# Placing the weight-decoding steps by the position within an expert in a fused attention, expert and feed-forward kernel

## Chip, core and metric

The kernel runs on one core of one Trainium2 chip, as one launch. The metric is the device time of that launch in microseconds. The engines that matter here are TensorE (matrix products), VectorE and ScalarE (elementwise work), GpSimd (elementwise work and gathers) and SyncE (which issues most of the transfers). Each engine works through its own list of instructions in order and waits at an instruction until what that one needs has arrived.

## What is computed

Three parts, one after the other, on 2304 tokens of width 512, in float32 (the weights of part 3 come in float64):

```python
# 1. attention with a decaying causal mask, 4 x 8 heads, 576 positions, head width 64
ret = scores * Dmat;  x = ret @ v                       # -> [2304, 512]
# 2. eight experts, one per token
expert_idx = argmax(xn @ en.T / tau)                    # one of 8
h = np.maximum(x[mask] @ w1[e], 0.0)                    # [tokens of e, 1024]
out[mask] = gate_w[mask, None] * (h @ w2[e])
# 3. feed-forward, d_ff 2048, weights given in float64
h = x @ w_in
g = np.where(h > 0.0, h, np.exp(np.minimum(h, 0.0)) - 1.0)
return g @ w_out
```

## The kernel before

**Precision.** Every product in parts 2 and 3 is made of three passes. A value is split into a high part `hi` (a rounded copy) and a low part `lo` (the rest), and `three` issues high x high, high x low and low x high.

**Expert loop.** The loop over `i` from 0 to 64 at the end of the listing below does part 2. Expert `e = i // 8` has its 1024 hidden units in eight slices, and `f = i % 8` is the place within the expert. In iteration `i`:

- `mm1(i)`: TensorE multiplies the tokens of the expert with slice `i` of `w1` (12 products). ScalarE then writes `hh`, the high part of the rectified result (L861), and VectorE `hl`, the low part (L862).
- `mm2(i-1)`: TensorE multiplies `hh`, `hl` of the slice before with its slice of `w2` into four accumulators `acc0` to `acc3` (12 products). The second product of the first accumulator reads `hl`. Where `i - 1` was the last slice of an expert, so in the iteration with `f` = 0, the results are taken: ScalarE copies each accumulator to `yh` (L878) and VectorE makes `yl` (L879), four times. The next expert's first `mm2` overwrites the accumulators, so it waits for these.
- for `f` = 4, 5, 6: `xpose` turns the next expert's gathered rows around (TensorE), with a copy on ScalarE (L839) and a subtraction on VectorE (L840).
- `split(i+2)`: the weights of slice `i + 2` are split, `ah` and `bh` on ScalarE (L208), `al` and `bl` on VectorE (L209).
- `decode(n)`: `n` steps of decoding, the subject of the change.

The instructions of each engine stand in this order. For VectorE the list of one iteration is thus: `hl`, then `yl` four times where `f` = 0, then the subtraction of `xpose` where `f` is 4 to 6, then `al` and `bl` for slice `i + 2`, and last the decoding steps. What the steps delay is `hl` of the next iteration and all that stands behind it.

**Decoding.** The weights of part 3 are float64 and are turned into float32 by whole-number arithmetic, in 32 blocks of 128 x 512, in the background of parts 1 and 2 and the start of part 3. A block takes four steps, each one instruction on VectorE: L145, L147, L150, L153. The second also issues a square on ScalarE (L148). The fourth also issues two transfers on SyncE: the load of the block after next, and the store of the finished block to the buffer `wd`. There are two blocks' buffers in turn. `decode(n)` runs the next `n` of the 128 steps, wherever the sequence stands.

**Gathers.** On GpSimd, `gather_expert` fetches the rows of the expert after next as soon as the transposes have freed the row buffers, in three pieces (L806), and multiplies each by its gates (L816, both inputs in on-chip memory).

**Where the steps go.** 12 steps run in part 1. In the expert loop an iteration runs `1 + (i % 3 == 1)` steps, for `i` up to 61: 83 in all. The remaining 33 run in part 3, from its loop over `j` (at most four an iteration).

Of the kernel before, what the change touches and what calls it, by code (L numbers as in the profile page):

```python
# [79 lines left out]
def tile_kernel(ctx: ExitStack, tc: tile.TileContext, q, k, v, emb, tau, w1, w2, w_in, w_out, const, out):  # L80
# [81 lines left out]
    def decode(n):  # L162
        for _ in range(n):
            next(dsteps, None)
# [654 lines left out]
    def gather_expert(e):  # L819
        if e < NE:  # L820
            i_, g_ = (ids0, gsl0) if e == 0 else (idsp[:, e], gslp[:, e])
            gather(e, lambda j: i_[:, j:j + 1], lambda j: g_[:, j:j + 1], e == 0)
# [3 lines left out]
    def xpose(key, j):  # L826
        if key not in rows:
            return
        if j == 0:
            xt[key] = [mp.tile([P, KD, CAPS[0]], F32R, tag=f"xt{a}", name=f"xt{a}_{key}")[:, :, :cap(key)] for a in "hl"]  # L830
        pt = pm.tile([P, KD, P], F32, tag="acc0" if (key, j) == (0, 2) else "tp", name=f"tp{key}_{j}", bufs=1 if (key, j) == (0, 2) else 2)
        o, m = subs(key)[j]
        for kk in range(KD):
            nc.tensor.transpose(pt[:, kk, :m], rows[key][j][:m, kk, :P], ident[:m, :m])
        h_, l_ = (t[:, :, o:o + m] for t in xt[key])
        if (key, j) == (0, 1):
            vec.tensor_copy(out=h_, in_=pt[:, :, :m])
        else:
            nc.scalar.copy(out=h_, in_=pt[:, :, :m])  # L839
        low = lambda: vec.tensor_tensor(out=l_, in0=pt[:, :, :m], in1=h_.bitcast(F32), op=ALU.subtract)  # L840
        if key != 0:
            low()
        return low
# [3 lines left out]
    def mm1(i, key, w):  # L847
        hp = pm.tile([P, 512], F32, tag="h", name=f"h{i}", bufs=2)
        ah, al = w[:2]
        xh, xl = xt[key]  # L850
        c = cap(key)
        if i:
            for kk in range(KD):
                three(hp[:, :c], (ah[:, kk, :], al[:, kk, :]), (xh[:, kk, :], xl[:, kk, :]), kk == 0, kk == KD - 1)
        else:
            for l, r in ((ah, xh), (al, xh), (ah, xl)):
                for kk in range(KD):
                    nc.tensor.matmul(hp[:, :c], l[:, kk, :], r[:, kk, :], start=l is ah and r is xh and kk == 0, stop=r is xl and kk == KD - 1)
        hh = mp.tile([P, CAPS[0]], F32R, tag="hh", name=f"hh{i}")[:, :c]
        hl = mp.tile([P, CAPS[0]], F32R, tag="hl", name=f"hl{i}")[:, :c]  # L860
        nc.scalar.activation(out=hh, in_=hp[:, :c], func=AF.Relu)  # L861
        vec.scalar_tensor_tensor(out=hl, in0=hp[:, :c], scalar=0.0, in1=hh.bitcast(F32), op0=ALU.max, op1=ALU.subtract)  # L862
        hs[i] = (hh, hl)
# [3 lines left out]
    def mm2(i, f, key, w, ra, rv):  # L867
        c = cap(key)
        bh, bl = w[2:]
        if f == 0:  # L870
            for d in range(KD):
                acc[d] = pm.tile([P, 512], F32, tag=f"acc{d}", name=f"acc{i}_{d}")
        for d in range(KD):
            three(acc[d][:, :c], (bh[:, d, :], bl[:, d, :]), hs[i], f == 0, f == 7)
        if f == 7:
            ra, rv = ra(), rv()
            for d in range(KD):
                nc.scalar.copy(out=yh[d][:, bass.ds(ra, c)], in_=acc[d][:, :c])  # L878
                vec.tensor_tensor(out=yl[d][:, bass.ds(rv, c)], in0=acc[d][:, :c],  # L879
                                  in1=yh[d][:, bass.ds(rv, c)].bitcast(F32), op=ALU.subtract)  # L880

    def reg(eng, ap, top):
        return lambda: eng.value_load(ap, min_val=0, max_val=top)
# [11 lines left out]
    def compact():  # L895

        oe = qp.tile([P, NE], F32, name="oe")
        vec.tensor_tensor(out=ord_["t"], in0=ord_["perm"].rearrange("q p e -> q e p"),
                          in1=ord_["off"][:, :NE].unsqueeze(1).to_broadcast([P, NE, NE]), op=ALU.mult)
        vec.tensor_reduce(out=oe, in_=ord_["t"], axis=AX.X, op=ALU.add)  # L900
        t = qp.tile([P, NT, NE], F32, name="po1")
        pos = qp.tile([P, NT], F32, name="pos")
        pool.tensor_tensor(out=oe, in0=oe, in1=C("base"), op=ALU.subtract)
        rf = qp.tile([P, NT], F32, name="rf")
        pool.tensor_copy(out=rf, in_=rk)
        pool.tensor_tensor(out=t, in0=oh, in1=oe.unsqueeze(1).to_broadcast([P, NT, NE]), op=ALU.mult)
        vec.tensor_reduce(out=pos, in_=t, axis=AX.X, op=ALU.add)
        pool.tensor_tensor(out=pos, in0=pos, in1=rf, op=ALU.add)
        posi = qp.tile([P, 2, NT], I32, name="posi")
        posf = qp.tile([P, 2, NT], F32, name="posf")  # L910
        pool.tensor_copy(out=posi[:, 0, :], in_=pos)
        vec.tensor_scalar(out=posi[:, 1, :], in0=posi[:, 0, :], scalar1=127, scalar2=None, op0=ALU.bitwise_and)
        vec.tensor_scalar(out=posi[:, 0, :], in0=posi[:, 0, :], scalar1=7, scalar2=None, op0=ALU.arith_shift_right)
        pool.tensor_copy(out=posf, in_=posi)
        return posf
# [4 lines left out]
    def compact_part(k, posf):  # L920
        bt = qp.tile([P, CK, P], BF16, tag="cb", name=f"cb{k}", bufs=3)
        at = qp.tile([P, CK, NPART, NT], BF16, tag="ca", name=f"ca{k}", bufs=3)
        for j in range(CK):
            n = k * CK + j
            o18 = qp.tile([P, NT], BF16, name=f"co{n}", tag="co", bufs=2)
            pool.tensor_scalar(out=bt[:, j, :], in0=C("i128"), scalar1=posf[:, 1, n:n + 1], scalar2=None, op0=ALU.is_equal)
            pool.tensor_scalar(out=o18, in0=C("i128")[:, :NT], scalar1=posf[:, 0, n:n + 1], scalar2=None, op0=ALU.is_equal)
            pool.tensor_tensor(out=at[:, j], in0=o18.unsqueeze(1).to_broadcast([P, NPART, NT]),
                               in1=parts[:, n, :].unsqueeze(2).to_broadcast([P, NPART, NT]), op=ALU.mult)
        cparts[k] = (bt, at)  # L930

    def compact_sum(k):
        if k == 0:
            cparts["pc"] = pm.tile([P, NPART, NT], F32, tag="tp", name="pc", bufs=2)
        bt, at = cparts[k]
        for j in range(CK):
            n = k * CK + j
            nc.tensor.matmul(cparts["pc"].rearrange("p a b -> p (a b)"), bt[:, j, :], at[:, j].rearrange("p a b -> p (a b)"),
                             start=n == 0, stop=n == NT - 1)

    def compact_end():
        pc = cparts["pc"]
        cid = qp.tile([P, 2, NT], F32, name="cid")
        for j, (lo, hi) in enumerate(((0, 2), (2, NPART))):
            vec.tensor_reduce(out=cid[:, j, :], in_=pc[:, lo:hi].rearrange("p a b -> p b a"), axis=AX.X, op=ALU.add)
        vec.tensor_copy(out=idc, in_=cid[:, 0, :])
        cparts["cid"] = cid
# [62 lines left out]
    for i in range(NI1 + 1):  # L1010
        if i < NI1:
            mm1(i, i // 8, splits[i])
        if i:
            e, f = divmod(i - 1, 8)
            ap = offi[0:1, e:e + 1]
            mm2(i - 1, f, e, splits[i - 1], reg(nc.scalar, ap, N) if e else lambda: 0, reg(vec, ap, N) if e else lambda: 0)
        e, f = divmod(i, 8)
        if i < NI1:
            if f == 0 and e:
                gather_expert(e + 1)  # L1020
            if 4 <= f < 7:
                xpose(e + 1, f - 4)
        if i == 9:
            posf = compact()
        if 9 <= i < 21 and i % 4 == 1:
            compact_part((i - 9) // 4, posf)
        if i in (26, 27, 28):
            compact_sum(i - 26)
        if i == 28:
            compact_end()  # L1030
        if i == 29:
            compact_store()
            rest = rest_table(ord_["off"], ord_["cnp"])
        if 30 <= i < 46 and i % 2 == 0:
            next(rest, None)
        if i == 46:
            n_trips = nc.values_load(trips[0:1, 0:1], min_val=0, max_val=NK)
        if i < NI1 - 1:
            split(i + 2)
        if i < NI1 - 2:  # L1040
            decode(1 + (i % 3==1))


    qctx.close()
# [142 lines left out]
```

## Time and profile before

| what | value |
|---|---|
| median of three runs | 776.66 us (776.53 to 778.18) |
| profiled execution | 775.07 us, of which the span from first to last instruction is 772.6 us |
| mean granted TensorE clock | 0.993 of full speed |
| TensorE busy | 746.9 us, 97% of the span |
| VectorE busy | 501.1 us, 65% |
| ScalarE busy | 431.4 us, 56% |
| GpSimd busy | 183.2 us, 24% |
| expert loop | about 125 to 358 us of the span |
| part 3 | from about 361 us to the end |

A busy share is a sum over stages with different limits. TensorE is nearly always busy, so only time in which it stands still can be won. Where that happens, the profile names the instruction that it waited for. Times in a timeline are microseconds from the start of the span.

### The profile page before, as it was taken

The page shows a single profiled execution, that of the slowest core. Times are in us where ns is not written, and L with a number is a line of the kernel's source. Part 1 is how long each engine was busy: PE and PEld are TensorE (multiplying, and loading weights), DVE is VectorE, ACT ScalarE, POOL GpSimd, SP SyncE. Part 2 cuts the span into 40 slices and gives each one's busy share as a digit, 9 for nine tenths or more (in the row PEclk, how much of TensorE's full clock was granted, in tenths as well). Part 3 has the DMA queues.
Part 4 walks back from the last instruction along what each step waited for, and adds up shares of the span by engine and source line. Part 5 has one row for each costly group of instructions (what it writes and reads, how often), then busy time and mean ns, then how long its engine had stood idle before and what let it go on. Part 6 is the DMA issues. An engine that isn't in the chain of part 4 may idle for free.

```text
span 772.6 us, 13379 instructions
## 1 busy us (share of the span) xinstructions
PE 746.9 (97%) x5048; PEld 691.0 (89%) x5049; DVE 501.1 (65%) x975; ACT 431.4 (56%) x857; POOL 183.2 (24%) x291
## 2 busy tenths in 40 slices
PE   8899978999999999998999999999999999999996
PEld 7898966999999999998888998998899899899895
DVE  4365667697888897895887655555555555554553
ACT  3555543455455555565766555655555565565552
POOL 4466656259922533000000000030000003000003
PEclk9999998999999999999999999999999999999999
DMA  8989836575686668494432422050202205020002
GB/s 205 258 218 243 242 129 208 196 248 206 224 280 201 243 217 305 165 323 157 144 143 83 145 102 109 1 191 1 110 11 98 109 1 190 1 110 1 0 1 81
DMA packets 92266, 113.91 MB, mean 147 GB/s; under 512 B 59514, under 2 KB 59806, under 8 KB 89126
## 3 DMA queue, kind: packets, MB, share of 16 engines
q1 hardware_dynamic: 87654, 100.90, 39.9%
q0 software_dynamic: 3104, 9.83, 3.9%
q10 hardware_dynamic: 1440, 2.29, 0.8%
q8 instruction: 41, 0.67, 0.3%
q14 instruction: 27, 0.22, 0.1%
HBM read 95.16 MB, written 17.84 MB: 146 GB/s over the span
## 4 chain that ended last, share of the span: by engine, by line
PE 35%; issue 15%; POOL 2%; ACT 1%; DVE 0%; POOLq 0%; DVEq 0%
PE h L220 6%; PE h L221 6%; PE h L219 6%; PE o L221 6%; PE o L219 6%; PE o L220 6%; POOL out_dram L1144 1%; POOLq L1183 0%; DVE gl L1119 0%; POOL nil L1143 0%; ACT gh L1118 0%; DVE bl L209 0%; ACT ah L208 0%; ACT bh L208 0%; DVE g L1113 0%
## 5 line engine op out<-in xcount | busy, mean ns | idle before, releaser
L1111 DVE SCALAR_TENSOR_TENSOR ex<-ex,th 128x384 f32<-128x384 f32 x96 | 53.6, 558 | 124.7 <-ACT th L1110 124.7
L219 PE MATMUL h<-yh,ah 128*128 128x384 f32 x384 | 129.5, 337 | 2.6 <-DVE bl L209 2.6
L220 PE MATMUL h<-yl,ah 128*128 128x384 f32 x384 | 130.5, 340 | 0.0
L221 PE MATMUL h<-yh,al 128*128 128x384 f32 x384 | 129.5, 337 | 0.0
L221 PE MATMUL o<-bh,gl 128*128 128x512 f32 x288 | 114.0, 396 | 0.2
L219 PE MATMUL o<-bh,gh 128*128 128x512 f32 x288 | 114.0, 396 | 0.0
L220 PE MATMUL o<-bl,gh 128*128 128x512 f32 x288 | 113.7, 395 | 0.0
L1144 POOL DMA_INDIRECT out_dram<-ob,idc x18 | 19.2, 1064 | 387.0 <-ACT ob L1141 383.4
L1105 ACT ACTIVATE r<-h 128x384 f32<-128x384 f32 x96 | 47.1, 490 | 89.3 <-PE h L221 85.4
L208 ACT CAST bh<-rawb 128x512 fp32r<-128x512 f32 x112 | 69.7, 623 | 28.7 <-PE acc L220 22.0
L209 DVE TENSOR_TENSOR bl<-rawb,bh 128x512 fp32r<-128x512 f32 x112 | 81.3, 726 | 6.0 <-ACT bh L208 5.6
L209 DVE TENSOR_TENSOR al<-rawa,ah 128x512 fp32r<-128x512 f32 x112 | 80.6, 719 | 3.6 <-ACT ah L208 3.1
L220 PE MATMUL acc<-hl,bh 128*128 128x342 f32 (+7 forms) x256 | 78.0, 305 | 1.9 <-DVE hl L862 1.7
L219 PE MATMUL h<-xth,ah 128*128 128x332 f32 (+7 forms) x252 | 78.5, 312 | 0.1
L219 PE MATMUL acc<-hh,bh 128*128 128x342 f32 (+7 forms) x256 | 77.9, 304 | 0.1
L221 PE MATMUL acc<-hh,bl 128*128 128x342 f32 (+7 forms) x256 | 77.6, 303 | 0.0
L221 PE MATMUL h<-xth,al 128*128 128x332 f32 (+7 forms) x252 | 76.5, 304 | 0.8 <-DVE al L209 0.8
L220 PE MATMUL h<-xtl,ah 128*128 128x332 f32 (+7 forms) x252 | 76.4, 303 | 0.0
L219 PEld LDWEIGHTS h<-yh,ah 128*128 128x128 f32 x384 | 72.0, 187 | 4.8 <-ACT bh L208 2.8
L220 PEld LDWEIGHTS h<-yl,ah 128*128 128x128 f32 x384 | 72.1, 188 | 2.1
L1118 ACT CAST gh<-g 128x768 fp32r<-128x768 f32 x48 | 40.1, 835 | 59.6 <-DVE g L1115 54.7
L221 PEld LDWEIGHTS h<-yh,al 128*128 128x128 f32 x384 | 72.7, 189 | 0.0
(228 smaller groups left out, 1513.3 us busy)
## 6 DMA issues: line engine op xcount, KB each, us to landing
rawa<-in_moe_w_dram SPq DMA_DIRECT2D x15, 1024.0 KB, 5.6
rawb<-in_moe_w_dram SPq DMA_DIRECT2D x15, 1024.0 KB, 7.3
rawa<-wd SPq DMA_DIRECT2D x12, 1024.0 KB, 4.7
rawb<-wd SPq DMA_DIRECT2D x12, 1024.0 KB, 6.6
draw<-in_moe_w_in_dram SPq DMA_DIRECT2D x16, 512.0 KB, 5.6
wd<-db SPq DMA_DIRECT2D x32, 256.0 KB, 3.7
draw<-in_moe_w_out_dram SPq DMA_DIRECT2D x16, 512.0 KB, 8.6
q<-in_q_dram SPq DMA_DIRECT2D x16, 256.0 KB, 3.8
```

The lines of the kernel that those rows point to most:

```text
L208: nc.scalar.copy(out=hi, in_=src)
L209: nc.vector.tensor_tensor(out=lo, in0=src, in1=hi.bitcast(F32), op=ALU.subtract)
L219: nc.tensor.matmul(o, lh, rh, start=first, stop=False)
L220: nc.tensor.matmul(o, lh, rl, start=False, stop=False)
L221: nc.tensor.matmul(o, ll, rh, start=False, stop=last)
L1105: nc.scalar.activation(out=r, in_=hp, func=AF.Relu, scale=-1.0)
L1111: vec.scalar_tensor_tensor(out=ex, in0=ex, scalar=1.0, in1=th, op0=ALU.add, op1=ALU.mult)
L1118: nc.scalar.copy(out=gh, in_=g)
L1144: ins = pool.indirect_dma_start(out=out[:, :], out_offset=bass.IndirectOffsetOnAxis(ap=idc[:, col:col + 1], axis=0), in_=ob, in_offset=None)
```

## The change

The number of decoding steps of an iteration is taken from the place `f` within the expert and no longer from `i % 3`. An expert gets 0, 1, 2, 2, 1, 1, 2, 2 steps at `f` = 0 to 7, which is 11, where it got 10 or 11. Over `i` = 0 to 61 the loop runs 84 steps, one more than before, and part 3 gets 32, one fewer.

```diff
         if i < NI1 - 1:
             split(i + 2)
         if i < NI1 - 2:
-            decode(1 + (i % 3==1))
+
+            decode((0, 1, 2, 2, 1, 1, 2, 2)[f])
```

## Rows read from the trace of the kernel before

**Rows 1.** Busy by stage: window, length, PE, PEld, DVE, ACT, POOL, clock, DMA share, GB/s.
```profile
246.98:275.26 28.28, 28.28 (x207) 28.04 (x205) 25.86 (x48) 16.52 (x34) 14.17 (x21) 1.00 0.77 269
...
370.00:770.00 400.00, 396.12 (x1967) 356.29 (x1966) 228.78 (x370) 234.15 (x439) 20.61 (x35) 1.00 0.21 79
```

**Rows 2.** Waits of TensorE, 125 to 358 us: total, times, longest.
```profile
PE acc L220 <- DVE hl L862: 1.7, 2, 1.0
...
PE h L221 <- DVE al L209: 0.8, 2, 0.6
```

**Rows 3.** Groups of VectorE instructions, 125 to 357 us: the four decoding steps.
```profile
L153 DVE SCALAR_TENSOR_TENSOR db<-dsq,db 128x512 f32<-128x512 f32 x20 | 15.4, 771 | 0.0
L147 DVE SCALAR_TENSOR_TENSOR db<-draw,db 128x512 int32<-128x512 int32 x21 | 15.4, 732 | 0.0
L150 DVE SCALAR_TENSOR_TENSOR db<-draw,db 128x512 int32<-128x512 int32 x21 | 14.6, 696 | 0.7
...
L145 DVE TENSOR_SCALAR db<-draw 128x512 int32<-128x512 int32 x21 | 9.0, 427 | 0.0
```

**Rows 4.** Timeline (start, duration), expert 2: VectorE, GpSimd, TensorE.
```profile
195.07 2.08 DVE L209 TENSOR_TENSOR al<-rawa,ah 128x512 fp32r<-128x512 f32 x1
...
199.97 0.47 DVE L862 SCALAR_TENSOR_TENSOR hl<-h,hh 128x312 fp32r<-128x312 f32 x1
...
195.53 1.06 POOL L816 TENSOR_TENSOR row<-row,gslp 128x512 f32<-128x512 f32 x1
...
200.49 0.41 PE L220 MATMUL acc<-hl,bh 128*128 128x312 f32 x1 [1.00 <-DVE hl L862]
```

**Rows 5.** Timeline, ends of experts 0 and 3: VectorE, GpSimd, TensorE.
```profile
156.89 0.50 DVE L862 SCALAR_TENSOR_TENSOR hl<-h,hh 128x342 fp32r<-128x342 f32 x1
...
157.88 0.31 PE L220 MATMUL acc<-hl,bh 128*128 128x342 f32 x1
...
247.79 0.41 DVE L145 TENSOR_SCALAR db<-draw 128x512 int32<-128x512 int32 x1
248.12 0.46 DVE L862 SCALAR_TENSOR_TENSOR hl<-h,hh 128x304 fp32r<-128x304 f32 x1
...
251.41 1.61 DVE L879 TENSOR_TENSOR yl<-acc,yh 128x304 f32 x4
...
251.71 1.03 POOL L816 TENSOR_TENSOR row<-row,gslp 48x512 f32<-48x512 f32 x1 [4.41 <-DMA row<-xd,idsp]
...
248.80 0.30 PE L220 MATMUL acc<-hl,bh 128*128 128x304 f32 x1
...
252.00 0.34 PE L219 MATMUL acc<-hh,bh 128*128 128x302 f32 x1
```

**Rows 6.** Timeline, end of expert 4: VectorE, GpSimd, TensorE.
```profile
277.38 0.45 DVE L862 SCALAR_TENSOR_TENSOR hl<-h,hh 128x302 fp32r<-128x302 f32 x1
...
278.96 0.41 DVE L145 TENSOR_SCALAR db<-draw 128x512 int32<-128x512 int32 x1
...
279.67 1.61 DVE L879 TENSOR_TENSOR yl<-acc,yh 128x302 f32 x4
...
281.79 0.67 DVE L209 TENSOR_TENSOR al<-rawa,ah 128x512 fp32r<-128x512 f32 x1
...
278.11 2.16 POOL L816 TENSOR_TENSOR row<-row,gslp 32x512 f32<-32x512 f32 x1 [3.02 <-DMA row<-xd,idsp]
...
277.90 0.39 PE L220 MATMUL acc<-hl,bh 128*128 128x302 f32 x1
...
281.13 0.30 PE L219 MATMUL acc<-hh,bh 128*128 128x292 f32 x1
...
283.02 0.30 PE L221 MATMUL h<-xth,al 128*128 128x292 f32 x1
```

**Rows 7.** Timeline, end of expert 5: VectorE, TensorE.
```profile
307.69 1.53 DVE L153 SCALAR_TENSOR_TENSOR db<-dsq,db 128x512 f32<-128x512 f32 x1
...
310.00 0.40 PE L219 MATMUL acc<-hh,bh 128*128 128x282 f32 x1
```

## Prediction

> **What bounds the kernel now.** I read the busy time by stage first, then the waits of TensorE, then the timelines around each of those waits. The reader should see three things in that order.
>
> First, TensorE sets the time and has little left to give. In the window of expert 4 (about 28.3 us) it is busy throughout, at a granted clock of 1.00, while VectorE is busy 25.86 of 28.28 us. In part 3 TensorE is busy 396.12 of 400 us with VectorE at 228.78 [rows 1]. So VectorE is near its limit in the expert loop and far from it in part 3.
>
> Second, in the whole expert loop TensorE waits for VectorE only a little: 1.7 us in two waits for `hl`, 0.8 us in two for `al` [rows 2]. Those 2.5 us are 0.3% of the run, and no placement of the decoding steps can win much more than that, since the steps themselves cost TensorE nothing.
>
> Third, these waits come where GpSimd multiplies gathered rows. In expert 2 an `al` that began at 195.07 took 2.08 us, while GpSimd multiplied at 195.53 for 1.06 us. Elsewhere an `al` takes 0.67 us [rows 6]. The queue behind it brings `hl` to 199.97, and TensorE waits 1.00 us for it [rows 4]. A multiply on GpSimd therefore holds VectorE up by about its own length.
>
> [...]
>
> **The change part by part.**
>
> *The number of steps.* The loop runs 84 instead of 83, part 3 runs 32 instead of 33. A step is 0.43 us (L145) or 0.70 to 0.77 us [rows 3]. In part 3 this one step is hidden: VectorE has over 170 us free in the 400 us window [rows 1]. The last block is stored one step earlier, so the transfers that follow it are not later. I cost this at nothing. Without that cover it would be one step, 0.7 us at most, in the gaining direction. The steps' transfers are the same in number and move by an iteration or two; SyncE takes them in its order and TensorE is not waiting for any. I cost them at nothing too; if a load came late, the first step of a block would wait and hold `hl` like any other delay.
>
> *Steps removed at f = 0.* These stand behind `yl`, `al` and `bl` in VectorE's list. Removing them does not make the results of an expert come sooner. It relieves the iterations that follow. Two waits fall in such a place:
>
> - Expert 2, `hl` late by 1.00 us [rows 4]. At the iteration with f = 0 two steps ran (L147 and L150) and now none, so VectorE is up to 1.40 us ahead (2 x 0.70 [rows 3]). The wait goes: -1.0.
> - The shorter of the two waits for `al`. It lies in the second expert, two iterations behind an f = 0 that ran one step. 0.8 - 0.6 = 0.2 us [rows 2]; the rest of that group is the longest one, 0.6. One step, 0.70, covers it: -0.2.
>
> The 0.6 us wait and the second wait for `hl` (1.7 - 1.0 = 0.7 us) [rows 2] stand behind iterations f = 6 of experts 4 and 5, where a multiply of 2 us holds `al` or `bl` or the instruction before. The steps of those iterations come after `al`, and the two or three iterations before keep their number or are cut to a wait for the transposes. I leave both waits as they are: 0.
>
> *Steps added at f = 6 and 7.* What comes next there is `hl` of the last slices, and then `yl`, which must free the accumulators for the next expert. The slack is read as TensorE's start of the product that needs it minus VectorE's end:
>
> - End of expert 0, f = 6 runs two steps for one. `hl` ended at 156.89 + 0.50 = 157.39, and its product began at 157.88: slack 0.49 [rows 5]. One more step, 0.70: +0.2.
> - End of expert 3, f = 6 runs L145 and L147 where it ran L145. `hl` ended at 248.12 + 0.46 = 248.58, its product began at 248.80: slack 0.22 [rows 5]. One more step, 0.70: +0.5. The first `yl` (a quarter of 1.61, so near 0.45 for the first) ended near 251.86, the accumulator's product began at 252.00: slack 0.14 [rows 5]. TensorE is 0.5 later by then and `yl` 0.7: +0.1.
> - End of expert 4, f = 6 runs L153 and L145 where it ran L153. L145 costs 0.34 from its start to the next, as 247.79 to 248.12 shows [rows 5]. `hl` ended at 277.83, its product began at 277.90: slack 0.07 [rows 6]. +0.3. At f = 7 two steps (L147, L150: 1.40) replace L145 (0.34). `yl` is then 0.34 + 1.06 = 1.40 later in all. It ended near 279.67 + 0.45 = 280.12 and was needed at 281.13, by then 281.4: +0.1. `al` behind it ended at 282.46 and was needed at 283.02, by then 283.4: it ends at 283.86, +0.5. At f = 0 the two removed steps give the 1.40 back, so the delay ends there.
> - End of expert 5, f = 7 runs L145 and L147 where L153 ran, which was held to 1.53 us by a multiply. The accumulator's product at 310.00 already stood behind it [rows 7]. If the multiply runs beside L145, the new pair costs about 0.1 more than the held L153, and if L145 is held first, 0.4 to 0.5. I take 0.3.
>
> At the ends of experts 1, 2 and 6 TensorE waits for nothing now [rows 2]; no multiply holds up VectorE there at f = 6, so I cost them at 0, with one step, 0.7, as the upper bound. The last expert has no next one to make room for.
>
> *Sum.* -1.2 + 0.2 + 0.6 + 0.9 + 0.3 = +0.8 us.
>
> *What is unknown.* At the ends of experts 3 and 4 a third multiply, for the last piece of the rows, comes at 251.71 and 278.11 [rows 5, 6]. At 278.11 it came while `al` ran, took 2.16 us instead of 1.03, and delayed nothing on VectorE: it lost to the three instructions that stood there back to back. In expert 5 it won, and L153 took 1.53 instead of about 0.7 [rows 3, 7]. With two steps of two inputs each in the place of L145, the one at 278.11 finds one more gap. If it wins, `yl` is 1.03 later. The cost of a hit is thus between 0 and 1.03 at each of the two places. It is nearest to the row of expert 5, which is the same instruction at the same place: that one cost VectorE 0.8. I take a quarter of one hit, 0.2.
>
> So the forecast is +1.0 us. It is made against the profiled execution: 775.07 + 1.0 = 776.1. The median of the runs shown is 1.59 us above that execution, so the median becomes 776.66 + 1.0 = **777.7 us**.
>
> **The rivals.**
>
> *Slower: the multiplies catch the added steps.* Both third multiplies win against a step, at experts 3 and 4. The place is f = 7, where VectorE now has two steps between `bl` and `hl`. For it: expert 5 shows just that [rows 7]. Against it: expert 4 before shows the multiply losing three times [rows 6], and `hl` and `yl` read accumulators and were not stretched. It decides where one hit of 1.03 passes the slack that the delayed `yl` has left, which is near zero at both places. Price: 0.8 + 1.03 + 1.03 = +2.9, so 779.5 us. With one full hit it is +1.8, 778.5 us.
>
> *Faster: the added steps find cover.* Here `hl` at the ends of experts 3 and 4 is not what TensorE meets late, because the two-microsecond multiplies at f = 6 hit VectorE while it is idle and no longer while it works on `al` and `bl`. It decides where that gives `hl` 0.5 us more slack than the 0.22 and 0.07 of now. Then only the gain of 1.2 stands, and the 0.6 us wait for `al` in expert 4, made by the same holding, goes as well: -1.8, so 774.9 us. For it: idle time and work alternate within a few tenths of a microsecond. Against it: the multiplies follow the transposes of f = 4 to 6, which the change does not move, and `al` follows them too.
>
> *It does not do what it says.* The steps vanish at f = 0, but `yl` stands ahead of them in the list, so the freed time falls to the iterations after. If, moreover, the queue is empty by f = 1 anyhow, both gain and loss shrink to the waits of single places: between -0.5 and +0.5, about 776.7 us. Against it is the 1.00 us wait of expert 2, which stands behind two steps at f = 0 [rows 4].
>
> **How the numbers follow.** This kernel's runs differ by 0.2% (776.53 to 778.18), and about 0.2%, 1.55 us, is what can be told from no change. Chances: my forecast of +0.3 to +1.5 us 0.38, the slower rival 0.34, the faster one 0.12, the one without effect 0.16. The forecast and the last rival lie within 0.2%, though a little of the forecast reaches over: same 0.53. Slower is 0.35, faster 0.12. The range leaves out the end of the faster rival and the double hit's upper end: 776.66 - 1.1 to 776.66 + 2.9, so 775.6 to 779.6 us. My likeliest case alone is 777.0 to 778.2.
>
> **What would show it.** Right: the wait of 1.00 us for `hl` in expert 2 is gone; TensorE has new waits of some tenths for `hl` at the ends of experts 3 and 4 and for `yl` at the start of experts 4, 5 and 6; the 0.6 us for `al` in expert 4 and 0.7 us for `hl` in expert 5 are still there; part 3 is as long as before. Wrong: the sum of TensorE's waits in the loop falls well below 2.5 us, or rises over 5; a step waits for its load; or part 3 changes.

## The result, and the profile after

The changed kernel takes **781.37 us**, median of 8 runs (779.04 to 784.50), against 775.80 us (773.00 to 778.18, 8 runs) for the kernel before: ratio 1.0083, 95% interval 1.0059 to 1.0106. It is slower by 5.6 us. The prediction was 777.7 us with a range to 779.6, so the time lies above the range. It had added 1.0 us to 776.66, the median of the first three of the runs before. The profiled execution took 779.89 us with a span of 778.1.

The loss is not mainly in the loop that was changed. I cut both spans at the starts of the same three products, read from TensorE's timeline: one of the first layer early in the loop (the thirteenth with `xth`), the last one into `acc`, and the first of part 3 (`h<-yh`). Times are us.

| | before | after | difference |
|---|---|---|---|
| up to the first cut | 129.24 | 128.83 | -0.4 |
| expert loop | 228.79 | 230.55 | +1.8 |
| pause at the conditional | 2.86 | 4.95 | +2.1 |
| part 3 to the end | 411.73 | 413.76 | +2.0 |
| span | 772.6 | 778.1 | +5.5 |

The conditional is `tc.If(n_trips > 0)`, which stands between the loop and part 3 (L1047 before, L1048 after; it guards passes for overflowing experts, which this input doesn't take). The prediction does not mention it. TensorE's timeline there, after:

```profile
359.38 0.29 PE L221 MATMUL acc<-hh,bl 128*128 128x276 f32 x1
364.33 0.66 PE L219 MATMUL h<-yh,ah 128*128 128x384 f32 x1 [4.66 <-SPq L1048]
```

Before, the same two products start 2.86 us apart:

```profile
358.03 0.29 PE L221 MATMUL acc<-hh,bl 128*128 128x276 f32 x1
...
360.89 0.41 PE L219 MATMUL h<-yh,ah 128*128 128x384 f32 x1 [2.58 <-DVE bl L209]
```

The releaser in the brackets differs, and neither name is the cause, as the branch itself will show below. Busy time by stage (length, then PE, PEld, DVE, ACT and POOL busy, the granted clock, the DMA share, GB/s): loop, pause, the 10.7 us behind it, and 400 us of part 3, after:

```profile
127.00:359.40 232.40, 228.78 (x1631) 223.97 (x1629) 196.00 (x345) 130.32 (x265) 90.16 (x122) 1.00 0.68 238
359.40:364.30 4.90, 0.27 (x3) 0.04 (x1) 2.46 (x6) 1.83 (x4) 0.00 (x0) 0.76 0.53 206
364.30:375.00 10.70, 10.67 (x49) 10.70 (x50) 2.60 (x5) 4.63 (x10) 0.09 (x1) 0.79 0.01 2
375.00:775.00 400.00, 396.59 (x1969) 356.33 (x1967) 228.48 (x369) 234.16 (x440) 20.64 (x35) 1.00 0.21 78
```

The pause and what follows it, before:

```profile
358.00:360.90 2.90, 0.32 (x4) 0.13 (x2) 2.51 (x6) 1.88 (x4) 0.09 (x1) 1.00 0.04 17
360.90:371.60 10.70, 10.55 (x56) 9.90 (x57) 4.67 (x8) 6.66 (x15) 0.00 (x0) 1.00 0.17 51
```

Two things are to be seen. In the pause the DMA engines are busy at a share of 0.53, where it was 0.04. Behind it the granted clock is 0.79, where it was 1.00: 49 products in 10.7 us for 56. The trace after has two levels there, 0.50 from 362.0 to 368.8 and 1.00 from then on; products of 384 columns start 0.32 us apart in the first stretch (from the second one on) and 0.17 to 0.18 in the other. The other 400 us of part 3 run as before [rows 1]. So the +2.0 us of part 3 goes with the clock that fell in the longer pause; e4 below tests that.

In the loop, TensorE's waits are these (line, waited for: us in total, times, longest). After:

```profile
PE acc L220 <- DVE hl L862: 1.3, 3, 0.7
PE acc L219 <- DVE yl L879: 1.3, 3, 0.6
PE h L221 <- DVE al L209: 0.8, 2, 0.6
```

Before, in the same stretch, `hl` has 1.7 us, `al` 0.6 in one wait, and `yl` none. The second wait for `al` in [rows 2] lies ahead of this stretch.

### The profile page after: what moved, and what is told of

It is laid out like the page before. It is cut to its first block, busy times and chain, and to the rows that moved or that the text cites. A ratio compares the mean times of both kernels' runs of the same rounds, so it can differ in the third digit from the quotient of the medians.

```text
span 778.1 us, 13382 instructions
## 1 busy us (share of the span) xinstructions
PE 750.7 (96%) x5048; PEld 694.2 (89%) x5049; DVE 503.4 (65%) x975; ACT 431.7 (55%) x857; POOL 185.8 (24%) x291
## 4 chain that ended last, share of the span: by engine, by line
PE 35%; issue 15%; POOL 2%; ACT 0%; DVE 0%; POOLq 0%
PE h L220 6%; PE h L219 6%; PE h L221 6%; PE o L221 6%; PE o L219 6%; PE o L220 6%; POOL out_dram L1145 1%; POOLq L1184 0%; DVE gl L1120 0%; POOL nil L1144 0%; ACT gh L1119 0%; ACT bh L208 0%; DVE ex L1112 0%; DVE g L1114 0%; ACT ob L1142 0%
```

## The experiments

There were two questions. **Which half of the edit lengthens the pause**: the new order over f, or the 84th step in the loop? And **what is the pause**: TensorE waiting for something on VectorE or SyncE that the added step delays, or something of the conditional itself? The table gives the three stages of each profiled execution (cut as above), and beside them TensorE's branch at the conditional and the 16 KB instruction load that falls within it (queue q8; start of its packets), all in us of that execution. Each row is one execution, and those of e3, e5, e6, e7 and e10 took 1.0 to 2.0 us longer than the medians of their kernels, so what a kernel costs is read from the medians below. The texts on the expectations were written before each run.

| kernel | loop | pause | part 3 | branch, start to end | load, start to end |
|---|---|---|---|---|---|
| before | 228.79 | 2.86 | 411.73 | 356.31 - 360.26 | 357.82 - 358.78 |
| after | 230.55 | 4.95 | 413.76 | 357.64 - 363.63 | 361.24 - 362.23 |
| e1 | 229.78 | 2.90 | 411.74 | 359.01 - 363.01 | 360.57 - 361.53 |
| e2 | 227.89 | 5.71 | 414.49 | 354.41 - 361.15 | 358.80 - 359.81 |
| e3 | 229.92 | 3.90 | 413.10 | 358.64 - 363.64 | 361.31 - 362.33 |
| e4 | 229.93 | 5.31 | 411.71 | 360.03 - 364.48 | 362.02 - 363.10 |
| e5 | 230.64 | 5.23 | 414.25 | 359.98 - 366.24 | 363.78 - 364.76 |
| e6 | 228.47 | 4.53 | 413.26 | 359.61 - 365.16 | 362.72 - 363.82 |
| e7 | 227.12 | 3.27 | 413.21 | 356.40 - 360.69 | 358.37 - 359.36 |
| e8 | 230.11 | 0.13 | 411.62 | none | none |
| e9 | 227.70 | 2.59 | 413.28 | 354.60 - 358.22 | 355.62 - 356.75 |
| e10 | 229.09 | 2.33 | 411.76 | 358.60 - 362.02 | 359.61 - 360.65 |
| e11 | 229.96 | 2.46 | 413.28 | 356.92 - 360.46 | 357.93 - 359.06 |
| e12 | 227.53 | 0.13 | 411.62 | none | none |

**e1: the new order with 83 steps.**

```
-            decode((0, 1, 2, 2, 1, 1, 2, 2)[f])
+            decode((0, 1, 2, 2, 1, 1, 2, 2)[f] if i < NI1 - 3 else 0)
```

> The changed kernel with the last step of the expert loop (the 84th, at i = 61) left to part 3, so that 83 steps run in the loop as before. Join theory (the two transfers issued by the 84th step hold up all engines at the conditional behind the loop, and TensorE's clock falls in that pause): the pause of 4.95 us at the conditional goes back to about 2.9, the clock stays at 1.00 behind it, and only the loop's own loss of some 1.3 us remains: ratio to before 1.001 to 1.003. Loop theory (the steps moved to f = 6 and 7 cost nearly all of it): the loss stays, ratio 1.007 to 1.009.

776.98 us against 774.77 on the same chip: 1.0031 [1.0012, 1.0050]. The pause is 2.90 us and part 3 411.74, as before; the loop stays long (229.78).

**e2: the old order with 84 steps.**

```
-            decode(1 + (i % 3==1))
+            decode(1 + (i % 3==1) + (i == NI1 - 3))
```

> The kernel before with one step more at i = 61 and everything else as it was: 84 steps in the loop, spread by i % 3. Join theory: the loop's waits are those of before, the pause at the conditional grows from 2.9 to about 5 us and the clock falls behind it; ratio to before 1.004 to 1.007. Loop theory: no change that can be measured, ratio 0.999 to 1.001.

778.92 us, 1.0064 [1.0042, 1.0087]. One more step in the last iteration that decodes, and nothing else, gives a pause of 5.71 us and a part 3 of 414.49, with a loop no longer than before. Its pause and the stretch behind it:

```profile
356.15:361.86 5.71, 0.29 (x3) 0.09 (x2) 2.48 (x6) 1.85 (x4) 0.09 (x1) 0.94 0.40 148
361.86:372.50 10.64, 10.64 (x45) 10.64 (x46) 2.23 (x4) 3.85 (x9) 0.00 (x0) 0.71 0.01 2
```

The two kernels split the loss: the order lengthens the loop, the 84th step the pause and, through the clock, part 3. What does that step bring? It is the L153 of block 23, the only one of the four steps that issues transfers. SyncE's timeline after:

```profile
352.21 0.32 SPq L183 DMA_DIRECT2D rawa<-wd  x1
353.31 0.72 SPq L183 DMA_DIRECT2D rawb<-wd  x1
354.08 1.04 SPq L134 DMA_DIRECT2D draw<-in_moe_w_in_dram  x1
355.21 0.51 SPq L155 DMA_DIRECT2D wd<-db  x1
```

Before, the two loads of unit 17 (L183; they fetch the second set of part 3's weights, `rawa` and `rawb`) stood there as well (350.86 and 351.96), but the other two came later:

```profile
360.00 0.35 SPq L134 DMA_DIRECT2D draw<-in_moe_w_in_dram  x1
371.96 0.32 SPq L155 DMA_DIRECT2D wd<-db  x1
```

The draw load stood 0.3 us ahead of the end of TensorE's branch, behind its instruction load, and the store 11.1 us behind the pause. Now they are issued 3.6 and 2.4 us ahead of the branch's start.

**e3: the 84th step stays, its two transfers go behind the conditional.**

```
-            decode_load(i + 2)
-            nc.sync.dma_start(out=wd[u][m][:, kk * 512:(kk + 1) * 512], in_=b1.bitcast(F32))
...
+            def moves(i=i, u=u, m=m, kk=kk, b1=b1):
+                decode_load(i + 2)
...
+            if i == 23:
+                later.append(moves)
+            else:
+                moves()
...
+    for go_ in later:
+        go_()
     split(NI1 + 1)
```

> The changed kernel with all its 84 steps, but the load and the store of the 84th step are issued behind the conditional. It tells the transfers from the VectorE instruction. Join theory with the transfers as the cause: as with 83 steps, ratio to before 1.001 to 1.003, pause about 2.9 us. If the instruction itself were the cause, or the loop: 1.006 to 1.009.

777.82 us, 1.0046 [1.0026, 1.0065], and a pause of 3.90 us. In this execution that undoes half of the added pause, not all, and by the medians 3.0 us over before are left of after's 5.6 (e1: 2.2), although the two transfers are now issued at 362.40 and 362.85, when the instruction load in the table has already ended. The transfers matter, then, but they are not alone in flight: the loads of unit 17 (1024 KB each) stand 5.4 us ahead of TensorE's branch, in e3 as before.

**e4: TensorE kept busy in the pause** (18 products into an unused tile ahead of the conditional; nothing reads them).

```
+    t = pm.tile([P, 512], F32, tag="tp", name="warmi", bufs=2)
+    for _ in range(18):
+        nc.tensor.matmul(t, lowb, oneb.unsqueeze(1).to_broadcast([P, 4, P]), start=True, stop=True)
     qctx.close()
```

> The changed kernel with 18 products on TensorE added behind the loop, whose result is read by nobody, to fill most of the pause at the conditional (about 4 us of it). The pause itself is not shortened. If the lower clock behind the pause costs about 2 us, the granted clock stays at 1.00 and the time falls by about 2 us against the changed kernel: ratio to before 1.004 to 1.007. If the clock costs nothing: ratio as the changed kernel, 1.008.

778.37 us, 1.0054 [1.0035, 1.0074]. The pause is no shorter than after's, 5.31 us, most of it filled with those products; the clock holds, and part 3 is back at 411.71:

```profile
359.90:365.20 5.30, 4.18 (x22) 1.77 (x20) 2.46 (x6) 1.83 (x4) 0.09 (x1) 1.00 0.36 135
365.20:375.90 10.70, 10.56 (x56) 9.91 (x57) 4.68 (x9) 6.67 (x15) 0.00 (x0) 1.00 0.01 2
```

The +2.0 us of part 3 is thus the clock, and with TensorE at work in the pause the clock does not fall. The pause itself does not depend on it.

**e5: e3, and the loads of unit 17 written behind the conditional too. e6: the kernel before, with only those loads moved.**

```
-        load_wanted()
+        if i not in (4 * NU1 - 1, 4 * NU1):
+            load_wanted()
```

> The changed kernel with its 84 steps; the 84th step's two transfers and also the two loads of weight unit 17 (rawa and rawb, 1 MB each, issued some 6 us before the conditional) are issued behind it, so that no large transfer is under way when the engines branch. Two theories of the pause are left after the first four runs. Fetch theory (TensorE's branch waits for a load of instructions, and that load queues behind data transfers): the branch becomes much shorter than the 3.9 to 6.7 us seen so far, the load of instructions starts at once, the pause falls to 2.9 us or less, the clock holds, ratio to before 1.001 to 1.003 (the loop's loss is left). Join theory (SyncE's waits for the transfers set the end of the pause): the pause falls too, but TensorE's branch keeps its length.

> The kernel before with the two loads of weight unit 17 issued behind the conditional, its steps untouched. Fetch theory: TensorE's branch, 3.94 us before, gets shorter, and the pause of 2.86 us falls by up to 1 us; ratio 0.997 to 1.000. Join theory: SyncE ended its waits 0.3 us after the last VectorE result, so at most 0.3 us is won; ratio 0.999 to 1.000.

e5 took 781.39 us, 1.0075 [1.0051, 1.0099]; e6 778.96 us, 1.0056 [1.0036, 1.0076]. Neither did what was expected: e5 lost no less than after, 7.1 us, and e6, which has the steps of before, lost 4.6 us, with pauses of 5.23 and 4.53 us. The edits did not do what they were meant to. The conditional's line in e6, and SyncE's timeline (the duration of each branch in ns, smallest, median and largest, then its start):

```profile
L1048 SPq COMPARE_BRANCH  x1: 53/53/53, 350.1 to 350.1; - x1
L1048 PEldq COMPARE_BRANCH  x1: 5552/5552/5552, 359.6 to 359.6; - x1
```

```profile
354.17 0.33 SPq L183 DMA_DIRECT2D rawa<-wd  x1
355.27 0.40 SPq L183 DMA_DIRECT2D rawb<-wd  x1
356.63 0.33 SPq L134 DMA_DIRECT2D draw<-in_moe_w_in_dram  x1
```

SyncE passed its own branch 9.5 us ahead of TensorE's, and issued the "later" loads 5.4 us ahead of that, just as before (350.86 against a branch at 356.31). What moved is the draw load: before, SyncE issued it at 360.00, behind the loads and behind its waits at the conditional, which last to 359.9; here SyncE is through the conditional already (its waits there end at 353.6) and issues it at 356.63, 3.0 us ahead of TensorE's branch. In e5 the loads of unit 17 came 3.3 and 2.8 us ahead of the branch and the two transfers of block 23 6.5 and 3.7, also still ahead. A place in the program is no time. But the failures tell something: one more transfer issued just ahead of the branch, here without an 84th step, and the pause is longer.

**What the pause is.** The same view after (GpSimd passed its own branch at 308.8, in 54 ns):

```profile
L1048 SPq COMPARE_BRANCH  x1: 53/53/53, 355.8 to 355.8; - x1
L1048 PEldq COMPARE_BRANCH  x1: 5982/5982/5982, 357.6 to 357.6; - x1
L1048 ACTq COMPARE_BRANCH  x1: 54/54/54, 359.7 to 359.7; - x1
L1048 DVEq COMPARE_BRANCH  x1: 72/72/72, 360.1 to 360.1; - x1
```

The branch costs these other engines 53 to 72 ns and TensorE 5982 ns. It begins at 357.6, while products issued earlier still run, and ends at 363.63; the first product starts 0.70 us later. Before, it takes 3942 ns, in e2 6742:

```profile
L1047 PEldq COMPARE_BRANCH  x1: 3942/3942/3942, 356.3 to 356.3; - x1
```

The waits of SyncE at the conditional do not set the end of the pause: they last to 364.2 after, but in e6 and e9 they end at 353.6 and 348.7, 11.6 and 9.5 us ahead of the end of TensorE's branch, and in all twelve executions with a conditional the first product follows that end by 0.63 to 0.71 us. In each of them the branch ends 1.3 to 1.5 us after the end of a 16 KB load on an instruction queue (table). What differs is when that load starts: 1.5 us behind the branch before, 3.6 after, 4.4 in e2. The DMA queues (packets, MB, share), after, from the branch to the load's start, and then to the branch's end:

```profile
q1 hardware_dynamic: 270, 1.39, 96.8%
q14 instruction: 1, 0.01, 0.5%
...
q1 hardware_dynamic: 142, 0.27, 29.8%
q8 instruction: 1, 0.02, 2.5%
```

The data queue fills the first stretch to 96.8%, with 1.39 MB; the load on q8 comes when it has thinned out. Before, the same two stretches:

```profile
q1 hardware_dynamic: 71, 0.52, 82.9%
...
q1 hardware_dynamic: 18, 0.07, 7.2%
q8 instruction: 1, 0.02, 2.4%
```

The other executions with data in flight go the same way. From the branch to the load's start q1 moves 0.52 MB in e1 (1.6 us), 0.62 in e4 (2.0), 0.76 in e7 (2.0), 0.69 in e3 (2.7), 1.13 in e6 (3.1), 1.37 in e5 (3.8) and 1.35 in e2 (4.4). In all nine that is 82 to 99% of what q1 moves within the whole branch, so the load comes when nearly all that was in flight is through. The order by size is not strict, and why e3 and e7, with the same loads issued as early as before, had 0.69 and 0.76 MB left for 0.52, the traces do not tell.

In each of TensorE's twelve long branches there is one load of 16 KB on q8, and the branch ends 1.3 to 1.5 us behind its end. What the load brings, the traces do not show, and that TensorE waits for it is my reading of these times.

**e8 and e12: no conditional**, in the changed kernel and in the one before (`with tc.If(n_trips > 0):` becomes `if False:`; the overflow passes are left out).

> The changed kernel, 84 steps and transfers in place, without the conditional behind the loop: it leaves out the passes for tokens that exceed an expert's capacity, which the conditional guards. If the conditional is what turns the 84th step's transfers into a pause, the pause falls to 1.5 to 2.5 us (the taking of the last results), the clock holds, and the time is 4 to 6 us below the changed kernel: ratio to before 1.000 to 1.003. If the transfers delay TensorE by themselves (part 3's first products): no change, 1.008.

> The kernel before without the conditional (it leaves out the passes for tokens beyond an expert's capacity). Beside the changed kernel without it (0.9987 of before) this tells the loop's part of the loss alone, free of the pause and of the clock. If the order of the steps costs some 1.9 us in the loop, as the lengths of the loop in the profiled executions say: ratio 0.995 to 0.997, so 1.5 to 2.5 us below the changed kernel without it. If the order costs nothing that lasts: 0.998 to 1.000.

e8: 773.55 us, 0.9987 [0.9972, 1.0001]. e12: 771.46 us, 0.9942 [0.9920, 0.9964]. In both the pause is 0.13 us (I had expected 1.5 to 2.5 in e8), and e8 issues the two transfers of the 84th step no later than after does, 5.5 and 4.9 us ahead of the last product into `acc` (after: 5.3 and 4.2). Nor is there a load on q8 at this place: the nearest ones in e8 start at 353.5 and 373.7. TensorE in e8:

```profile
360.60 0.29 PE L221 MATMUL acc<-hh,bl 128*128 128x276 f32 x1
360.73 0.34 PE L219 MATMUL h<-yh,ah 128*128 128x384 f32 x1
```

So the added transfers delay no data that TensorE needs. They delay the branch, and without the branch no pause comes of them. Between e8 and e12 only the order and the 84th step differ: loops of 230.11 and 227.53 in the profiles, 2.1 us between the medians (3.3 if each is set against the before of its own chip).

**e9, e10, e11: transfers truly held back.** The loads of unit 17 are called behind the conditional and made to wait there for a small write on VectorE into the tile that each fills; VectorE reaches it only after its own branch (at 357.1 in e9; SyncE issues the first of these loads at 358.07). e9 is the kernel before, e11 the changed kernel with the two transfers of block 23 behind the gated loads, e10 the changed kernel with another spread of 83 steps (e7, next).

```
-    def load_unit(u, eng=None):
+    def load_unit(u, eng=None, gate=False):
...
             for t, m in ((a, 0), (b, 1)):
+                if gate:
+                    nc.vector.memset(t[0:1, 0, 0:1], 0.0)
                 nc.sync.dma_start(out=t, in_=wd[(u - NU1) % 4][m].rearrange("p (k f) -> p k f", k=4))
...
+    load_unit(want.pop(0), gate=True)
     split(NI1 + 1)
```

> The kernel before, its steps untouched, with the two loads of weight unit 17 really later: they are issued behind the conditional and wait for a small write by VectorE that stands behind the last results, so SyncE can't issue them before about 359 us, when TensorE is already at its branch. (In the two runs before, SyncE passed the conditional ahead of the others and issued them early.) Fetch theory: TensorE's load of instructions starts within about 1 us of the branch, the branch takes some 2.5 to 3 us for 3.94, the pause 1.4 to 1.9 us for 2.86, the clock holds; ratio to before 0.997 to 0.999. If the branch does not depend on data transfers: branch 4 us, ratio 1.000.

> The changed kernel, same 84 steps at the same places, with the loads of unit 17 gated and the 84th step's load and store issued behind them, so that nothing large is under way when TensorE branches. Fetch theory: pause 1.4 to 1.9 us, no fall of the clock, and what remains against before is the loop's loss of 1 to 2 us less the 1 us won at the pause: ratio 1.000 to 1.003, which is 5 us or more below the changed kernel. If the 84 steps cost by themselves: 1.006 to 1.009.

> Steps 0, 2, 2, 2, 2, 1, 1, 1 with 83 in the loop, and the loads of unit 17 gated as in the run beside it. The loop is some 1 to 1.5 us shorter than before, the pause 1.4 to 1.9 us, no fall of the clock: ratio to before 0.994 to 0.998, so a kernel faster than both. If the fetch theory is wrong the pause stays at about 3 us with or without a fall of the clock: 0.998 to 1.002.

e9: 774.45 us, 0.9988 [0.9970, 1.0005]. e10: 774.70, 0.9993 [0.9972, 1.0013]. e11: 776.83, 1.0026 [1.0006, 1.0046]. In e9 and e11 no packet moves between the start of the branch and that of the load, and in e10 SyncE issues no transfer from 350 us to 362.05. In all three the load starts 1.0 us behind the branch: branches of 3.4 to 3.6 us, pauses of 2.33 to 2.59. That is shorter than before's 2.86, but not the 1.4 to 1.9 expected. In e9 the clock fell all the same, to a mean of 0.84 in the 10.7 us behind the pause (1.00 in e10), and part 3 took 413.28 us; e11 has the same 413.28, which I take for such a fall, though its clock by stage was not read. e11 has 84 steps and the new order, and loses 2.0 us where after lost 5.6. In e9, the branch, and the queues from its start to the load's, which hold nothing at all, and then to its end:

```profile
L1050 PEldq COMPARE_BRANCH  x1: 3617/3617/3617, 354.6 to 354.6; - x1
...
DMA packets 0, 0.00 MB, mean 0 GB/s; under 512 B 0, under 2 KB 0, under 8 KB 0
...
q8 instruction: 1, 0.02, 2.6%
q14 instruction: 1, 0.01, 1.0%
```

**e7: another spread of 83 steps**, none at f = 0 and one each at f = 5 to 7.

```
-            decode((0, 1, 2, 2, 1, 1, 2, 2)[f])
+            k = min((0, 2, 2, 2, 2, 1, 1, 1)[f], 83 - done)
+            done += k
+            decode(k)
```

> The steps by place again, but 0, 2, 2, 2, 2, 1, 1, 1 for f = 0 to 7 and at most 83 in the loop, so that f = 6 and 7 run one step each and the 84th is left to part 3. If the two steps at f = 6 and 7 are what costs in the loop, the new waits for hl and yl at the ends of experts 0, 3, 4 and 5 go, the loop is as long as before or up to 1 us shorter, and the pause is as before: ratio 0.997 to 1.001. If fewer steps at f = 0 is itself the loss: 1.002 to 1.004, as with 83 steps of the changed order.

776.09 us, 1.0017 [0.9996, 1.0039]. Its loop, 227.12 us, is the shortest of all: the waits for `yl`, and those for `hl` at the ends of experts 3 and 4, are gone. Its pause of 3.27 us and a part 3 of 413.21 take that back; the length is that of e9, so I take it for a fall of the clock, which was not read by stage here. With the gate, e10's pause is 2.33 and part 3 411.76, but that execution's loop has 229.09, so two executions of one order can be 2.0 us apart in the loop. Neither can be told from the kernel before, and none of these kernels that keeps the conditional is clearly faster than it.

## Why the prediction was wrong

**The step that failed** is *the number of steps*: "The last block is stored one step earlier, so the transfers that follow it are not later. I cost this at nothing", and on the transfers "TensorE is not waiting for any". The transfers are indeed not later, but the price of nothing does not follow: counted from the loop's last product they are issued 7 and 18 us earlier, and so stand ahead of TensorE's branch. The second passage is wrong where it matters. TensorE waits for no data of theirs, as e8 shows, but it waits at the end of the loop for that branch, and the instruction load within it comes only when nearly all that is in flight is through (82 to 99% in nine executions): 3.6 us behind the branch's start, where it was 1.5. e1 against after puts the price of this step at about 3.4 us of the 5.6 (medians +2.2 and +5.6, each over the before of its own runs); e2 alone costs 4.2. In the profiled executions it is 2.1 us of pause and 2.0 of clock.

**The loop was mis-sized**: +0.8 us by its own sum, +1.0 with the weighed hit of a multiply, +1.8 in the profiled execution. Over the seven executions with the new order the loop has 229.78 to 230.64 us, mean 230.1; over the five with the old one 227.53 to 228.79, mean 228.1. The order costs about 2.0 us. Term by term, each wait read as the distance between the starts of two neighbouring products less the usual 0.155, and placed at the first of the two:

- *Waits removed, -1.2.* The wait of 1.0 us in expert 2 [rows 4] is gone, but it was that execution's own: e2, e6, e9 and e12 have the old order and do not have it there. Two of them have one in expert 3 instead (0.90 at 228.2 in e6, 0.21 in e2), the seven with the new order none. In the mean over the five such a wait is worth 0.5, not 1.0. The 0.2 for `al` was misread: the shorter wait of [rows 2] is not in the second expert but ahead of all steps that moved, and it stays (below). The place that was meant, at 167.1 before, has a wait of 0.23 to 0.25 in all five of the old order; it is still there in after and e5 (0.21 and 0.19) and gone in the other five. A wait of 0.3 us for `hl` at 284.4, which all five executions of the old order have, went; I had not foreseen that.
- *End of expert 0, +0.2*: 0.17 at 157.3. Right. A wait of 0.43 for `yl`, not foreseen, follows at 161.2; only after and e5 have it.
- *End of expert 3, +0.6*: 0.56, all of it `hl`; the 0.1 for `yl` did not come.
- *End of expert 4, +0.9*: `hl` 0.31 for 0.3 and `al` 0.30 for 0.5, but `yl` 0.75 for 0.1.
- *End of expert 5, +0.3*: 0.53, which was 0.22 before: +0.3. Right for this pair; over the executions 0.53 to 0.68 stands against 0.21 to 0.22 in four of the five and nothing in e12, +0.5 in the mean.

In the means over the two groups, -0.5, -0.2 and -0.3 for the waits removed and 0.2, 0.1, 0.6, 1.4 and 0.5 for those added make +1.8 of the 2.0; the rest is in distances too small to name. But for the `yl` at 161.2, the added waits repeat within 0.2 us in the seven executions. The misread wait, before and after, and two of the added ones, after (the brackets give the idle time and its releaser; they are shorter than the waits, since the record of the product ahead lasts 0.29 to 0.31 us and the usual distance is 0.155):

```profile
128.51 0.42 PE L221 MATMUL h<-xth,al 128*128 128x342 f32 x1 [0.15 <-DVE al L209]
...
128.10 0.42 PE L221 MATMUL h<-xth,al 128*128 128x342 f32 x1 [0.15 <-DVE al L209]
...
248.44 0.41 PE L220 MATMUL acc<-hl,bh 128*128 128x304 f32 x1 [0.41 <-DVE hl L862]
...
282.04 0.40 PE L219 MATMUL acc<-hh,bh 128*128 128x292 f32 x1 [0.61 <-DVE yl L879]
```

and in e8:

```profile
249.40 0.41 PE L220 MATMUL acc<-hl,bh 128*128 128x304 f32 x1 [0.41 <-DVE hl L862]
...
282.99 0.40 PE L219 MATMUL acc<-hh,bh 128*128 128x292 f32 x1 [0.59 <-DVE yl L879]
```

**The slower rival was half right.** At expert 4 the multiply caught an added step. VectorE and GpSimd, after:

```profile
279.11 0.67 DVE L147 SCALAR_TENSOR_TENSOR db<-draw,db 128x512 int32<-128x512 int32 x1
279.82 1.42 DVE L150 SCALAR_TENSOR_TENSOR db<-draw,db 128x512 int32<-128x512 int32 x1
...
281.54 1.59 DVE L879 TENSOR_TENSOR yl<-acc,yh 128x302 f32 x4
...
278.38 2.31 POOL L816 TENSOR_TENSOR row<-row,gslp 32x512 f32<-32x512 f32 x1 [3.47 <-DMA row<-xd,idsp]
```

L150 took 1.42 us for 0.70 [rows 3], beside a GpSimd multiply that began at 278.38 and took 2.31; `yl` starts at 281.54. That is one hit of 0.7 us, in all seven executions of the new order, where I had weighed 0.2. It is nearly the whole of the 0.75 for `yl`, and the largest part of what the loop's sum missed. At expert 3 there was none: the steps at f = 7, L150 and L153, took 0.68 and 0.69 at 249.51 and 250.23, and the multiply came behind them, at 250.85.

**Right** were the places of the new waits, but for the `yl` at the start of expert 4, which did not come, and that the 0.6 us for `al` in expert 4 and 0.7 for `hl` in expert 5 stay (275.2 and 306.6). The text also named the sign that would tell against it, "or part 3 changes"; it did. The faster rival is refuted: no cover was found.

**Open:** the clock. With TensorE idle it held at 1.00 through pauses of 2.33 (e10), 2.86 (before) and 2.90 us (e1) and the stretch behind them. In that stretch it fell to 0.84 in e9 (2.59), 0.79 after (4.95) and 0.71 in e2 (5.71). In e11 (2.46), e7, e3, e6 and e5 (3.27 to 5.23) only part 3 tells of it, with 413.10 to 414.25 us for 411.73. The pause's length alone does not decide, and no run here tells what does.

## What to carry to other kernels

A branch that all engines take was here a place of 3.4 to 6.7 us in TensorE's schedule: look how long each engine's own branch lasts and what is in flight when TensorE's begins. Work that is "hidden" for its arithmetic may still move a transfer into such a place, so every DMA that a moved step issues needs its time of issue, ahead of the branch or behind it. And a wait that one execution shows is a gain only if another shows it too: waits that repeat over executions were worth counting here, the largest one was not.

## What was unexpected of the hardware

- TensorE's branch takes 3.5 and 3.6 us with nothing in flight (e11, e9) and 6.7 us behind 1.35 MB of data on q1 (e2); on the other engines listed above it takes 53 to 72 ns. The instruction load starts 1.0 us behind the branch with the data queue empty (e9, e11; also in e10, where SyncE issues nothing for 9 us ahead of it), 1.5 to 4.4 us behind it with data on it (nine executions).
- Where the granted clock fell, to a mean of 0.84 (e9), 0.79 (after) and 0.71 (e2) in the 10.6 to 10.7 us behind the pause, part 3 took 413.28, 413.76 and 414.49 us against 411.73 at 1.00 before; with products that nobody reads in the pause it stayed at 1.00 and part 3 took 411.71 (e4).
- SyncE runs through the conditional as soon as its own list allows, in e6 9.5 us ahead of TensorE, so a transfer written behind the conditional can be in flight when TensorE's branch begins.
